# Scores of the last queries in two 64x64 array tiles, and identity transposes on TensorE in the first steps of a fused attention and MLP kernel

## Chip, cores, metric

One core of one Trainium2 chip. The time is device microseconds of a whole execution, median of several executions. The kernel before takes 1509.5 us in the runs taken with the change. All runs quoted are of the fast state.

## The reference

```python
# threshold attention: q, k, v (8, 8, 576, 64), tau = 0.02
scores = np.matmul(q, k.transpose(0, 1, 3, 2)) / 8
thresh = np.max(scores, axis=-1, keepdims=True) - tau
scores = np.where(scores >= thresh, scores, -1e9)
attn = softmax(scores)
x = np.matmul(attn, v)                  # then (B,H,S,D) -> (4608, 512)
# MLP: w_in (512, 2048), w_out (2048, 512)
h = x @ w_in
out = np.maximum(h, 0) ** 2 @ w_out
```

All data are float32. Two heads of one batch are handled together as a pair, 64 head dimensions each, so a pair fills 128 partitions. The 576 queries of a head are four blocks of 128 and a rest of 64.

## The kernel before

One pair and one block of queries make a *step*. Step s computes scores (TensorE), their maximum (VectorE), the exponentials (ScalarE), the threshold (VectorE) and the division (GpSimd). Step s+1 transposes the weights of step s on TensorE (`turn`; in the last 8 of the 20 visits to a pair VectorE and DMA do it instead), and later steps multiply them with v (`mix`). MLP matmuls (`h`, `o`) are spread between steps from step 13 on. In the first 13 steps (`early()`) there is no such filling yet, and the MLP's weights are loaded and rounded.

For the rest of 64 queries (`i == NBLK`) both heads are put in one matmul on the whole array: `qmid` holds the queries of head 0 in one corner, those of head 1 in the other, zeros elsewhere.

```python
# prep(), part 0: q of a pair has been transposed
    if part == 0 and NBLK in visits[n][1]:
        for u in range(2):
            rows = slice(u * D, (u + 1) * D)
            nc.gpsimd.tensor_copy(out=qmid[n % 2][rows, u * D:(u + 1) * D], in_=qT[rows, NBLK * P:S])

def scores(vis, i):
    n = 2 if i < NBLK else 1
    sc = [psum.tile([P, 2, 512], FP32, tag=f"s{u}", name=f"s{u}") for u in range(n)]
    halves = [(half, u) for half in range(2) for u in range(n)]
    if early():
        halves.sort(key=lambda x: x[1])
    for half, u in halves:
        if i < NBLK:      # 64 x 128 tile of the array, head u in its half of the rows
            rows, lhsT = slice(u * D, (u + 1) * D), qT[u * D:(u + 1) * D, i * P:(i + 1) * P]
        else:             # whole array
            rows, lhsT = slice(0, P), qmid[vis % 2]
        nc.tensor.matmul(sc[u][:, half, 0:HALF], lhsT, kT[rows, half * HALF:(half + 1) * HALF], start=True, stop=True)
    # ... maximum, bias (tensor_scalar), thr (tensor_scalar), z on VectorE

# the loop over steps, cut
        scores(n, i)
        ...                          # exponents, rounding stages 1 and 2, prep of the next pair
        if s in mixes:
            mix(*mixes[s])
        ...
        fill(quarter)                # MLP matmuls; nothing in the early steps
        for part in range(3):
            turn(*steps[s - 1], part)
            if on and part == 0:
                threshold(n, i)
            if on and part == 1:
                divide(n, i)         # two tensor_scalar on GpSimd
            fill(quarter)
        if on:
            if now:
                end_rounding(now[0]) # one addition on GpSimd, then the next weight load
```

Of the kernel before, what the change touches and what calls it, by code (L numbers as in the profile page):

```python
# [9 lines left out]
FP32 = mybir.dt.float32  # L10
# [9 lines left out]
def kernel(  # L20
# [10 lines left out]
    nc = tc.nc  # L31
    B, H, S, D = q.shape
    d_model, d_ff = moe_w_in.shape
    n_tokens = out.shape[0]
    P = 128
    HP = H // 2
    NPAIR = B * HP
    NBLK = S // P
    REST = S - NBLK * P
    HALF = S // 2  # L40
# [9 lines left out]
    const = ctx.enter_context(tc.tile_pool(name="const", bufs=1))  # L50
    pool = ctx.enter_context(tc.tile_pool(name="work", bufs=2))
    psum = ctx.enter_context(tc.tile_pool(name="psum", bufs=1, space=bass.MemoryType.PSUM))

    ident = const.tile([P, P], FP32, name="ident")
# [9 lines left out]
    wT = const.tile([P, NC9, S], FP32, name="wT")  # L64

    vs = [const.tile([P, 2 * NBLK + 2, D], FP32, name=f"vs{i}") for i in range(2)]
    qmid = [const.tile([P, P], FP32, name=f"qmid{i}") for i in range(2)]
    for i in range(2):
        nc.gpsimd.memset(vs[i], 0.0)
        nc.gpsimd.memset(qmid[i], 0.0)  # L70



# [22 lines left out]
    def load_weights(i):  # L96
        nc.sync.dma_start(out=weight_area(i).bitcast(mybir.dt.int64), in_=weight_piece(i)[0])
# [29 lines left out]
    def load_qk(n):  # L127


        b, h = divmod(visits[n][0], HP)  # L130
        h *= 2
        tiles = []
        for name, t in (("ql", q), ("kl", k)):
            x = pool.tile([P, S // 32, 32], FP32, tag=name, name=name)
            for m in range(4):
                src = t[b, h + m // 2, :, (m % 2) * 32:(m % 2) * 32 + 32].rearrange("(c p) d -> p c d", p=32)
                last = REST // 32 if t is k and m >= 2 else 0
                to = x[m * 32:(m + 1) * 32, :, :]
                nc.sync.dma_start(out=to[:, last:, :], in_=src[:, 0:S // 32 - last, :])  # L139
                if last:  # L140
                    nc.sync.dma_start(out=to[:, 0:last, :], in_=src[:, S // 32 - last:, :])
            tiles.append(x)
        loaded[n] = tiles

    def load_v(n):
        b, h = divmod(visits[n][0], HP)
        h *= 2
        t = vs[n % 2]
        for u in range(2):
            at = u * (NBLK + 1)  # L150
            nc.sync.dma_start(out=t[:, at:at + NBLK, :],
                              in_=v[b, h + u, 0:NBLK * P, :].rearrange("(c p) d -> p c d", p=P))
            nc.sync.dma_start(out=t[u * D:(u + 1) * D, at + NBLK, :], in_=v[b, h + u, NBLK * P:S, :])

    def prep(n, part):

        if part == 0:
            ready[n] = [pool.tile([P, S], FP32, tag="qT", name="qT"), pool.tile([P, S], FP32, tag="kT", name="kT")]
        qT, kT = ready[n]
        nc.vector.transpose((qT, kT)[part], loaded[n][part].rearrange("p c d -> p (c d)"))  # L160
        if part == 0 and NBLK in visits[n][1]:
            for u in range(2):
                rows = slice(u * D, (u + 1) * D)
                nc.gpsimd.tensor_copy(out=qmid[n % 2][rows, u * D:(u + 1) * D], in_=qT[rows, NBLK * P:S])

    weights = {}

    def scores(vis, i):

        qT, kT = ready[vis]  # L170
        n = 2 if i < NBLK else 1
        sc = [psum.tile([P, 2, 512], FP32, tag=f"s{u}", name=f"s{u}") for u in range(n)]
        halves = [(half, u) for half in range(2) for u in range(n)]
        if early():
            halves.sort(key=lambda x: x[1])
        for half, u in halves:
            if i < NBLK:
                rows, lhsT = slice(u * D, (u + 1) * D), qT[u * D:(u + 1) * D, i * P:(i + 1) * P]
            else:
                rows, lhsT = slice(0, P), qmid[vis % 2]  # L180
            nc.tensor.matmul(sc[u][:, half, 0:HALF], lhsT, kT[rows, half * HALF:(half + 1) * HALF],  # L181
                             start=True, stop=True)
        st = pool.tile([P, 7, 2], FP32, tag="st", name="st", bufs=4)
        mx, bias, thr, z = (st[:, j, 0:n] for j in range(4))
        for u in range(n):
            nc.vector.tensor_reduce(out=mx[:, u:u + 1], in_=sc[u][:, :, 0:HALF], axis=AX.XY, op=ALU.max)  # L186
        nc.vector.tensor_scalar(out=bias, in0=mx, scalar1=-SCALE, scalar2=None, op0=ALU.mult)  # L187
        nc.vector.tensor_scalar(out=thr, in0=mx, scalar1=ntau8, scalar2=None, op0=ALU.add)


        nc.vector.tensor_tensor(out=z, in0=thr, in1=mx, op=ALU.is_gt)  # L191
        w = pool.tile([P, n, S], FP32, tag="w", name="w", bufs=3)
        weights[vis, i] = w, sc, st

    def exponents(vis, i):
        w, sc, st = weights[vis, i]
        for u in range(len(sc)):
            nc.scalar.activation(out=w[:, u, :].rearrange("p (h k) -> p h k", h=2), in_=sc[u][:, :, 0:HALF],  # L198
                                 func=AF.Exp, bias=st[:, 1, u:u + 1], scale=SCALE)
# [137 lines left out]
    visits = [(g, list(range(FIRST))) for g in range(HP)] + [(g, list(range(FIRST, NBLK + 1))) for g in range(HP)]  # L337
# [4 lines left out]
    def by_dma(n):  # L342

        return n >= 3 * HP
# [24 lines left out]
    def early():  # L369
        return state["step"] < min(chunk_at)  # L370

    def add_chunk(j):
        waiting.extend((IN_US, mlp_in, j, f, x) for f in range(NFT) for x in range(2))
        waiting.extend((OUT_US, mlp_out, j, t, x) for t in range(TCH // P) for x in range(NFT // OF))
# [14 lines left out]
    def fill(us):  # L389
        state["left"] += us  # L390
        while waiting and state["left"] >= waiting[0][0] / 2:
            cost, fn, *what = waiting.popleft()
            state["left"] -= cost
            fn(*what)
# [3 lines left out]
    for s, (n, i) in enumerate(steps):  # L398
        if s <= min(chunk_at) - 2:
            x = int(visits[n][1].index(i) != 1)  # L400
        else:
            x = 2 if n >= 2 * HP and i == NBLK else 1
# [5 lines left out]
    def end_rounding(p):  # L408
        round_weights(p, 3)
        if p + RAW < n_pieces:  # L410
            load_weights(p + RAW)

    load_qk(0)
    load_v(0)
    for i in range(RAW):
        load_weights(i)
    for part in range(2):
        prep(0, part)
    done = 0
    for s in range(END + 1):  # L420
        state["step"] = s
        on = s < NST
        now = []
        if on:
            n, i = steps[s]
            at = visits[n][1].index(i)
            now = list(range(done, done + pieces[s]))
            done += pieces[s]
            more = n + 1 < len(visits)
            short = len(visits[n][1]) <= FIRST  # L430
            if at == (0 if short else 1) and more:
                load_qk(n + 1)
            if now:
                round_weights(now[0], 0)
            scores(n, i)
            if now or early():
                exponents(n, i)
            if now:
                round_weights(now[0], 1)
                round_weights(now[0], 2)  # L440
            if short and at == 1 and more:
                prep(n + 1, 0)
                prep(n + 1, 1)
        if s in mixes:
            mix(*mixes[s])
        for j in chunk_at.get(s, ()):
            add_chunk(j)
        if 0 < s <= NST and by_dma(steps[s - 1][0]):
            m, x = steps[s - 1]
            turn_blocks(m, x)  # L450
            if x % 2 or x == NBLK:
                place_blocks(m, x // 2)
        quarter = rate(s) / 4 if s < END else 1e9
        fill(quarter)
        for part in range(3):
            if 0 < s <= NST and not by_dma(steps[s - 1][0]):
                turn(*steps[s - 1], part)
            if on and part == 0:
                if not (now or early()):
                    exponents(n, i)  # L460
                threshold(n, i)
            if on and part == 1:
                divide(n, i)
            fill(quarter)
        if on:
            if now:
                end_rounding(now[0])
            for p in now[1:]:
                for stage in range(3):
                    round_weights(p, stage)  # L470
                end_rounding(p)
            if not short and at == 3 and more:
                prep(n + 1, 0)
                prep(n + 1, 1)
            if more and at == len(visits[n][1]) - 1:
                load_v(n + 1)
# [32 lines left out]
```

## Time and profile before

| | before |
|---|---|
| median, lowest to highest of 4 | 1509.5 us, 1509.1 to 1509.7 |
| TensorE busy, of a span of 1507.6 us | 1443.9 us, 5504 instructions |
| 0 to 43, 43 to 107, 107 to 250 us: TensorE busy | 55, 75, 83% |
| from 250 us on | 99.7%, clock 1.00 |
| first h, first o | 107.0, 246.7 us |

A float32 matmul stands as two instructions in the trace, a transpose as one.

### The profile page before, as it was taken

Reading aid. Unit: us, or ns where it says so; the run is one execution under the profiler, and the core shown is the slowest. Engines: PE = TensorE matmul, PEld = TensorE weight load, DVE = VectorE, ACT = ScalarE, POOL = GpSimd, SP = SyncE. Lnnn points to the kernel's source line nnn. Section 1 sums busy time; section 2 is a strip of 40 time slices with the busy share of each in tenths; the row PEclk is TensorE's granted clock in tenths of the full one; section 3 lists DMA queues with packets and bytes.
Section 4 is the critical chain, followed back from the end, with each engine's and each line's share of the span. In section 5 each row is a group of like instructions: output and inputs, shape, how many; then the busy total and the mean of one; then the engine's idle time right before and its main releaser. Section 6 shows DMA issues by size and latency. Waiting matters only on the chain.

```text
span 1507.6 us, 17982 instructions
## 1 busy us (share of the span) xinstructions
PE 1443.9 (96%) x5504; PEld 756.2 (50%) x5504; DVE 824.8 (55%) x2049; ACT 414.4 (27%) x789; POOL 488.1 (32%) x619
## 2 busy tenths in 40 slices
PE   4788888999999999999999999999999999999998
PEld 3445445455455455455455455455455455455453
DVE  5779887346566665555556566565656565520000
ACT  3445554232122222122123122122223122111010
POOL 3456666124124233133133234133133223221020
PEclk9879989999999999999999999999999999999999
DMA  6345332114554454454554454444554454430000
GB/s 146 90 109 133 100 98 49 38 31 76 98 97 87 94 93 87 86 96 87 99 105 79 91 95 84 88 95 85 99 101 83 88 97 81 85 70 7 15 0 21
DMA packets 520255, 123.02 MB, mean 82 GB/s; under 512 B 511456, under 2 KB 511456, under 8 KB 520160
## 3 DMA queue, kind: packets, MB, share of 16 engines
q1 hardware_dynamic: 520128, 121.88, 41.6%
q8 instruction: 45, 0.74, 0.2%
q14 instruction: 50, 0.41, 0.1%
q0 software_dynamic: 32, 0.00, 0.0%
HBM read 48.63 MB, written 9.44 MB: 39 GB/s over the span
## 4 chain that ended last, share of the span: by engine, by line
PE 91%; DVE 6%; SPq 1%; issue 1%; ACT 0%; DMA 0%; DVEq 0%; ACTq 0%
PE o L326 34%; PE h L311 33%; PE s L181 13%; PE x_ps L289 11%; DVE st L186 2%; PE w_ps L229 1%; DVE cv L117 1%; DVE w L209 1%; SPq L139 1%; DVE cv L119 1%; DVE cv L116 1%; DVE st L187 0%; DVE st L191 0%; DVE kT L160 0%; ACT w L198 0%
## 5 line engine op out<-in xcount | busy, mean ns | idle before, releaser
L311 PE MATMUL h<-xT,w_in_sb 128*128 128x384 f32 x1536 | 523.8, 493 | 0.0
L326 PE MATMUL o<-w_out_sb,g 128*128 128x512 f32 x1152 | 515.3, 597 | 0.0
L186 DVE TENSOR_REDUCE st<-s 128x1 f32<-128x576 f32 x288 | 207.2, 753 | 394.9 <-PE s L181 394.9
L218 POOL TENSOR_SCALAR w<-w,st 128x576 f32<-128x576 f32 x288 | 233.9, 821 | 518.3 <-DVE st L212 499.3
L311 PEld LDWEIGHTS h<-xT,w_in_sb 128*128 128x128 f32 x1536 | 286.1, 191 | 205.2 <-issue 28.6
L326 PEld LDWEIGHTS o<-w_out_sb,g 128*128 128x128 f32 x1152 | 213.0, 190 | 256.8 <-issue 251.8
L316 POOL TENSOR_TENSOR g<-g 128x384 f32<-128x384 f32 x192 | 158.4, 826 | 375.7 <-ACT g L315 374.4
L198 ACT ACTIVATE w<-s,st 128x576 f32<-128x576 f32 x288 | 199.7, 742 | 272.3 <-DVE st L187 211.0
L209 DVE SCALAR_TENSOR_TENSOR w<-s,st,w 128x576 f32<-128x576 f32 x288 | 222.2, 804 | 57.5 <-ACT w L198 57.5
L181 PE MATMUL s<-kT,qT 64*128 64x288 f32 x1024 | 180.1, 453 | 39.5 <-DVE w L209 31.1
L315 ACT ACTIVATE g<-h 128x384 f32<-128x384 f32 x192 | 94.4, 492 | 323.5 <-PE h L311 323.4
L289 PE MATMUL x_ps<-wT,vs 128*64 128x320 f32 (+3 forms) x1280 | 174.9, 421 | 0.0
L181 PEld LDWEIGHTS s<-kT,qT 64*128 64x128 f32 x1024 | 101.2, 196 | 130.9 <-issue 96.7
L256 DVE STREAM_TRANSPOSE wb<-w 128x576 f32<-128x576 f32 x216 | 156.3, 757 | 17.7 <-DMA wT<-wb 9.7
L289 PEld LDWEIGHTS x_ps<-wT,vs 128*64 128x64 f32 x1280 | 88.3, 140 | 81.7 <-issue 34.9
L293 ACT COPY xT<-x_ps 128x256 f32<-128x256 f32 x48 | 17.9, 372 | 236.7 <-PE x_ps L289 236.7
L330 ACT COPY osb<-o 128x512 f32<-128x512 f32 x36 | 21.1, 587 | 176.9 <-PE o L326 98.7
L121 POOL TENSOR_TENSOR cv<-cv 128x512 f32<-128x512 f32 x32 | 40.8, 1274 | 78.0 <-DVE cv L119 65.7
L229 PE MATMUL w_ps<-ident,w 128*128 128x128 f32 x288 | 48.8, 306 | 7.1 <-ACT wT L230 6.9
L229 PEld LDWEIGHTS w_ps<-ident,w 128*128 128x128 f32 x288 | 37.8, 156 | 34.1 <-issue 13.9
L230 ACT COPY wT<-w_ps 128x384 f32<-128x384 f32 x96 | 42.4, 488 | 26.0 <-PE w_ps L229 25.9
L181 PE MATMUL s<-kT,qmid 128*128 128x288 f32 x128 | 37.6, 417 | 2.4 <-DVE w L209 2.4
(36 smaller groups left out, 457.8 us busy)
## 6 DMA issues: line engine op xcount, KB each, us to landing
wT<-wb SPq DMA_DIRECT2D x768, 72.0 KB, 2.2
ql<-in_q_dram SPq DMA_DIRECT2D x144, 72.0 KB, 2.5
vs<-in_v_dram SPq DMA_DIRECT2D x72, 128.0 KB, 2.5
out_dram<-osb SPq DMA_DIRECT2D x36, 256.0 KB, 2.2
area<-in_moe_w_in_dram SPq DMA_DIRECT2D x16, 512.0 KB, 3.9
area<-in_moe_w_out_dram SPq DMA_DIRECT2D x16, 512.0 KB, 3.6
kl<-in_k_dram SPq DMA_DIRECT2D x72, 72.0 KB, 2.5
kl<-in_k_dram SPq DMA_DIRECT2D x72, 64.0 KB, 2.3
```

The source lines that it names most:

```text
L181: nc.tensor.matmul(sc[u][:, half, 0:HALF], lhsT, kT[rows, half * HALF:(half + 1) * HALF], start=True, stop=True)
L186: nc.vector.tensor_reduce(out=mx[:, u:u + 1], in_=sc[u][:, :, 0:HALF], axis=AX.XY, op=ALU.max)
L198: nc.scalar.activation(out=w[:, u, :].rearrange("p (h k) -> p h k", h=2), in_=sc[u][:, :, 0:HALF], func=AF.Exp, bias=st[:, 1, u:u + 1], sc ...
L209: nc.vector.scalar_tensor_tensor(out=wu, in0=sc[u][:, :, 0:HALF], scalar=thr[:, u:u + 1], in1=wu, op0=ALU.is_ge, op1=ALU.mult, accum_out=s ...
L218: nc.gpsimd.tensor_scalar(out=w[:, u, :], in0=w[:, u, :], scalar1=z[:, u:u + 1], scalar2=rcp[:, u:u + 1], op0=ALU.add, op1=ALU.mult)
L229: nc.tensor.transpose(ps[:, n, :], w.rearrange("p u k -> p (u k)")[:, c * P:(c + 1) * P], ident)
L256: nc.vector.transpose(wb[:, u * KB:(u + 1) * KB, i % 2, :], w[:, u, :].rearrange("p (k q) -> p k q", q=32))
L289: nc.tensor.matmul(ps[u * D:(u + 1) * D, 0:nq], vs[n % 2][:, u * (NBLK + 1) + c, :], wT[:, cw, cols], start=(c == 0), stop=(c == NBLK))
L311: nc.tensor.matmul(h, w_in_sb[:, c, f * P:(f + 1) * P], xT[:, c, at:at + TCH], start=(c == 0), stop=(c == NMC - 1))
L315: nc.scalar.activation(out=g, in_=h, func=AF.Relu)
L316: nc.gpsimd.tensor_tensor(out=g, in0=g, in1=g, op=ALU.mult)
L326: nc.tensor.matmul(o, gs[j, f][:, t * P:(t + 1) * P], w_out_sb[:, f, :], start=(f == 0), stop=(f == NFT - 1))
```

## The change

It has two intents. The remaining queries need no copies into `qmid` and no multiplications with zeros, if each head's 64 queries use a 64x64 tile of the array, the two tiles side by side. And TensorE, half idle in the early steps, is kept at work with transposes of the identity so that its clock stays up.

```diff
-    qmid = [const.tile([P, P], FP32, name=f"qmid{i}") for i in range(2)]
...
-        if part == 0 and NBLK in visits[n][1]:
-            for u in range(2):
-                rows = slice(u * D, (u + 1) * D)
-                nc.gpsimd.tensor_copy(out=qmid[n % 2][rows, u * D:(u + 1) * D], in_=qT[rows, NBLK * P:S])
...
-        halves = [(half, u) for half in range(2) for u in range(n)]
+        halves = [(half, u) for half in range(2) for u in range(2)]
...
-            if i < NBLK:
-                rows, lhsT = slice(u * D, (u + 1) * D), qT[u * D:(u + 1) * D, i * P:(i + 1) * P]
-            else:
-                rows, lhsT = slice(0, P), qmid[vis % 2]
-            nc.tensor.matmul(sc[u][:, half, 0:HALF], lhsT, kT[rows, half * HALF:(half + 1) * HALF],
-                             start=True, stop=True)
+            rows = slice(u * D, (u + 1) * D)
+            to = sc[u] if i < NBLK else sc[0][rows]
+            nc.tensor.matmul(to[:, half, 0:HALF], qT[rows, i * P:min((i + 1) * P, S)],
+                             kT[rows, half * HALF:(half + 1) * HALF], start=True, stop=True)
...
+    def keep_busy(times):
+        idle = psum.tile([P, 4, P], FP32, tag="mm", name="idle", bufs=2)
+        for x in range(times):
+            nc.tensor.transpose(idle[:, x % 4, :], ident, ident)
+
     load_qk(0)
     load_v(0)
+    keep_busy(24)
...
         fill(quarter)
+        if 0 < s and early():
+            keep_busy(8)
         for part in range(3):
...
             fill(quarter)
+        if early():
+            keep_busy(8)
```

More of the change, by code (lines that the diff above doesn't have):

```diff
@@ L66 @@
     vs = [const.tile([P, 2 * NBLK + 2, D], FP32, name=f"vs{i}") for i in range(2)]
-    qmid = [const.tile([P, P], FP32, name=f"qmid{i}") for i in range(2)]
     for i in range(2):
         nc.gpsimd.memset(vs[i], 0.0)
-        nc.gpsimd.memset(qmid[i], 0.0)
     WP = 512
```

## The prediction

> **What bounds the kernel now.** I read the page first (busy shares and the 40 slices), then the busy time by stretches, the chain in order of time, and TensorE's timeline around single score groups.
>
> ```profile
> 0.00:43.00 43.00, 23.51 (x77) 15.39 (x79) 26.27 (x66) 14.89 (x26) 16.93 (x25) 1.00 0.62 141
> 43.00:107.00 64.00, 47.87 (x224) 28.58 (x221) 48.75 (x126) 31.81 (x62) 31.23 (x33) 0.76 0.42 98
> 107.00:250.00 143.00, 118.80 (x618) 69.84 (x617) 117.94 (x265) 77.29 (x157) 94.38 (x102) 0.92 0.42 105
> 250.00:1507.00 1257.00, 1253.72 (x4590) 642.38 (x4588) 631.84 (x1596) 290.39 (x546) 345.57 (x460) 1.00 0.41 76
> ```
>
> Columns: stretch, length, then busy us (instructions) of PE, PEld, DVE, ACT, POOL, then granted clock, DMA share, GB/s. There are two regimes. After 250 us PE is busy throughout at full clock: every added nanosecond of PE lengthens the run. Up to 107 us (the first 13 steps, where the code's `early()` holds for all but the last one) nobody is full, and the clock averages 0.76 in the second stretch. The 1.00 of the first stretch is no measurement: the clock's first record starts near 42.8 us, and the durations before it are those of half clock.
>
> ```profile
> 30.32 2.27 PE s L181 x6
> 32.61 1.51 DVE st L186 x2
> 35.07 0.70 DVE cv L117
> 36.23 0.74 DVE w L209 x2
> 37.11 3.00 PE s L181 x8
> 40.10 4.74 PE x_ps L289 x20
> 44.84 1.16 PE w_ps L229 x9
> 46.00 1.18 PE s L181 x8
> 47.20 1.43 DVE st L186 x2
> ```
>
> The chain (start, length) shows a ring: scores, maximum (L186), rounding and threshold on DVE, next scores, because the score buffers exist once. Scores cost 3.00 us cold and 1.18 warm; a plain step lasts 6.8 us cold (30.32 to 37.11), of which 2.3 us is the wait until head 0's scores are there, and 5.7 us warm. Where the ring meets a value product (x_ps), the link runs through PE alone.
>
> **What the Trainium skill says.** (1) "TensorE: Matmul & The Clock Gate", Part 1: half clock by default, full after about 3.4 us of busy time, half again after an idle window. The trace agrees and is sharper: all changes lie on one grid of 3.413 us (42.84, 53.08, 63.32, 73.56 ...). Every rise follows a window at least 0.88 full of matmuls; I divided PE's time in each window by line. (2) Same page, Part 4: a PE-mode transpose "doesn't count as PE-busy the same way". The trace agrees for the rise: the windows 73.56:76.97 and 94.04:97.45 were 100% busy, 1.74 and 1.30 us of that transposes (L229), and the clock stayed at 0.50. It disagrees for holding: 169.13:172.55 was busy for 1.64 us, 1.30 of them with transposes, and stayed warm, while 49.67:53.08, busy for 1.46 us and all of it matmuls, went cold. (3) "TensorEngine Tiling (Array Packing)", Key Properties: changing the tiling mode drains TensorE. The trace agrees; next fence. (4) Same page, Gotcha 1: different row tiles cannot write one PSUM bank at the same time. The matmuls of L241, in exactly the two diagonal 64x64 tiles and one bank, start 7 ns apart and leave 155 ns to the next, which is one 64-column slot (about 55 ns) and the switch: side by side works.
>
> ```profile
> 477.75 1.13 PE L181 MATMUL s<-kT,qmid 128*128 128x288 f32 x4
> 478.73 1.78 PE L311 MATMUL h<-xT,w_in_sb 128*128 128x384 f32 x5
> ...
> 411.60 1.24 PE L181 MATMUL s<-kT,qT 64*128 64x288 f32 x8
> 412.77 5.42 PE L326 MATMUL o<-w_out_sb,g 128*128 128x512 f32 x12
> 418.11 1.24 PE L181 MATMUL s<-kT,qT 64*128 64x288 f32 x8
> ```
>
> Start to start, four qmid instructions (two matmuls, an FP32 one counts twice) take 0.98 us, 243 ns each, and the h before and after keep their 322 ns. Eight tiled ones are four pairs, ideally 0.97 us too, but take 1.17; and twelve o between two tiled groups take 5.34 us instead of 12 x 0.429 = 5.15. So a visit to tiled mode costs 0.20 + 0.19 = 0.39 us on top.
>
> **Part 1: remaining queries in two tiles.** It removes 64 copies to qmid (15 us of POOL, not in the chain) and two memsets, and nothing from PE: two 128-row matmuls become two side-by-side pairs of equal streaming, four slots of 243 ns either way. The zero half of qmid cost no time. It adds the mode switch. Instruction by instruction the trace gives its four pieces: the last untiled instruction +94 ns (322 to 416), the first pair +104 with 128 weight columns but +50 with 64 columns (x_ps: 366 to 316), the last pair +97, the first untiled one after +104 (429 to 533). With 64 columns: 94 + 50 + 97 + 104 = 345 ns. After 250 us there are 26 such groups, 24 between untiled matmuls and 2 next to x_ps, which already pay one border (94 + 50 = 145 ns extra): 24 x 0.345 + 2 x 0.145 = 8.6 us, all on the path as PE is full. The other six lie before 250 us, where about half of PE's work is in the chain: 6 x 0.345 x 0.5 = 1.0 us. Sum: **+9.6 us**.
>
> **Part 2: the identity.** 24 transposes at the start, then 8 before and 8 after the transposes of w in steps 1 to 12. One takes 109 ns warm and 213 cold, start to start. The first 24 end by about 1.5 + 24 x 0.213 = 6.6 us, before the first scores at 8.45: free. They should not raise the clock, by (2). Then, by step:
> - Cold steps become PE-bound: scores 2.23 + 8 x 0.213 and a border 1.76 + nine w transposes 1.92 + eight more 1.70 + border 0.2 = 7.8 us against 6.8. Step 1 to 2: 2.93 + 1.76 + 1.92 + 1.70 + 0.2, so scores 2 start at 24.85, not 23.52. Scores 3 at 32.65 (before 30.32), scores 4 at 40.45 (37.11).
> - Step 4: scores to 42.7, x_ps cold until a window full of matmul ends, on the old grid 46.25; the remaining 4.5 pair slots of 0.32 end at 47.8, then 0.93 + 0.98 + 0.97 for the transposes. Scores 5 at 50.7, before 45.9: 4.8 us late.
> - From there the clock should hold: transposes fill what is idle. Plain steps last 5.7 us (DVE), value-product steps 2.0 + 3.4 + 0.93 + 0.98 + 0.97 = 8.3 us (PE, with 1.9 us of it identity). Scores 8 at 50.7 + 5.7 + 5.7 + 8.3 = 70.4 (before 66.9), 11 at 90.1 (87.6), 13 at 101.5 (100.1).
> - Step 13 then runs warm: 1.2 + 3.4 us instead of 2.2 + 4.4. Its x_ps ends near 106.2, before at 106.6. Sum: **-0.4 us**.
>
> The rest is paced by steps and follows this point one to one, so 1509.5 + 9.6 - 0.4 = 1518.7; I say **1518**, taking off a little for an early rise and for POOL relief.
>
> **Rivals.** (a) The identity also raises the clock, so all early steps are warm. Scores 2 still wait for the second k (landing near 21.9 us), so they start at 23.1; then 5.7, 5.7, 8.3 and so on put scores 13 at 93.8 and the end of its x_ps at 98.4, 8.2 us early: 1511. For it: pure transposes in a window were never seen. Against: the two full windows that stayed cold. (b) The identity neither raises nor holds. Then most steps stay at 7.8 us and more, and the 1.9 us of each PE-bound step comes on top; step by step the end of x_ps falls near 118.5, 12 us late: 1531. Against: the window 169.13:172.55, which transposes kept warm. (c) The diagonal tiles run one after the other: another 4 x 243 ns in each of 26 groups, 25 us: 1543. Against: L241. (d) Tiles without the cost of switching, with part 2 as I have it: 1509. Against: every tiled group in the trace pays it.
>
> **Range and chances.** I give my main course 0.65, (a) 0.15, (b) 0.1, the others and mixtures 0.1. The free grid and the five short cold spells between 107 and 250 us may move by some us either way. That gives 1510 to 1527. Two per cent are 30 us: faster 0.01, same 0.96, slower 0.03.
>
> **What would show it.** Right: score groups of remaining queries with 8 instructions, about 1.12 us from first to next start, 0.1 us more on each neighbour; the stretch from the first h (before 107 us) to the end some 9 us longer; no cold record between about 46 and 107 us; steps 2 to 4 later than before by 1.3 to 3.3 us, the first h within 2 us of before. A first h near 98 us would mean (a), one near 118 (b). Pairs of L181 243 ns apart instead of some 7 would mean (c). The number is wrong if the switch into 64x64 differs from that of L241, or if the early steps have a releaser that I took for hidden, such as a copy on ACT that frees the buffer of the identity.

## The result and the profile after

The changed kernel took 1524.15 us (1523.04 to 1525.02 in 4 executions), the kernel before 1509.51. The ratio is 1.0097, with a 95% interval of 1.0079 to 1.0114. Ratios here are the mean time of one kernel's fast runs over that of the other's of the same rounds, so not quite the ratio of the medians quoted. The sign and the class were foretold ("same": under 2%), and the range of 1510 to 1527 holds; the number was 6 us low.

Where the 13.7 us of the two traces lie is read from two marks. The first `h` came at 112.06 us instead of 107.01: 5.05 us are lost in the early steps. From the first `o` (251.85, before 246.72) to TensorE's last instruction it took 1265.57 us instead of 1257.01: 8.56 us more. Between the two marks nothing changed (139.79 and 139.71 us).

The same stretches as before, in the changed kernel:

```profile
0.00:43.00 43.00, 31.01 (x168) 23.19 (x169) 29.57 (x68) 14.88 (x26) 16.68 (x23) 0.88 0.60 141
43.00:107.00 64.00, 53.77 (x337) 38.36 (x337) 45.61 (x114) 30.78 (x60) 27.08 (x28) 0.89 0.38 84
107.00:250.00 143.00, 119.37 (x640) 67.88 (x639) 118.64 (x266) 75.21 (x152) 92.03 (x89) 0.91 0.47 111
250.00:1520.00 1270.00, 1267.42 (x4716) 635.74 (x4714) 635.96 (x1603) 293.45 (x551) 340.15 (x414) 1.00 0.41 75
```

In the second line the clock rose from 0.76 to 0.89 and PE is busier, yet DVE, whose work here is fixed, did only 45.6 us of it in the 64 us, where it had done 48.8. The clock went up and the steps went slower. The last stretch is full, as before.

TensorE's timeline around one group of remaining queries, now in tiles:

```profile
357.20 1.13 PE L304 MATMUL h<-xT,w_in_sb 128*128 128x384 f32 x3
358.26 1.19 PE L174 MATMUL s<-kT,qT 64*64 64x288 f32 x8
359.38 1.88 PE L304 MATMUL h<-xT,w_in_sb 128*128 128x384 f32 x5
```

Start to start the group takes 1.12 us (1.118 in the mean of 26 groups, before 0.977). Instruction by instruction the four pairs take 293, 243, 242 and 339 ns, the second of each pair 6 or 7 ns behind the first; the `h` ahead grew from 322 to 416 and the one behind to 427. These are the four pieces of the prediction.

The chain of work in two early steps of the changed kernel, 6 and 7:

```profile
51.37 1.25 PE s L174 x5
52.65 1.50 DVE st L179 x2
54.34 1.20 DVE st L181
...
57.32 0.75 DVE w L202 x2
58.11 3.02 PE s L174 x8
61.13 5.39 PE x_ps L282 x20
66.52 1.02 PE idle L410 x8
67.55 0.98 PE w_ps L222 x9
68.53 0.87 PE idle L410 x8
```

Scores at 51.37 are warm (1.25 us to the first head's end), those at 58.11 are cold again (3.02 us), and so is the value product behind them (5.39 us). Then 16 identity transposes follow in TensorE's own chain. And a tiny tensor_scalar, L181, on two columns, takes 1.20 us of the chain. Each of these has its own experiment below.

Where the early steps stood (start of the scores in us, from the traces). The last column is a run with the identity alone, described below:

| scores of step | before | predicted | changed | identity alone, low group |
|---|---|---|---|---|
| 2 | 23.5 | 24.9 | 23.5 | 23.3 |
| 4 | 37.1 | 40.5 | 35.9 | 35.8 |
| 5 | 45.9 | 50.7 | 45.8 | 44.0 |
| 8 | 66.9 | 70.4 | 69.3 | 64.4 |
| 11 | 87.6 | 90.1 | 93.1 | 84.9 |
| 13 | 100.1 | 101.5 | 105.5 | 97.3 |

Steps 1 to 4 came earlier than foretold, the steps with a value product (4, 7, 10: from one score to the next 9.8, 11.2, 11.4 us in the changed kernel) much later.

### The profile page after: what moved, and what is told of

Its sections match the earlier page's. It is cut to its first block, busy times and chain, and to the rows that moved or that the text cites. A ratio compares the mean times of both kernels' runs of the same rounds, so it can differ in the third digit from the quotient of the medians.

```text
span 1521.3 us, 18622 instructions
## 1 busy us (share of the span) xinstructions
PE 1471.6 (97%) x5856; PEld 765.2 (50%) x5856; DVE 829.8 (55%) x2049; ACT 414.3 (27%) x789; POOL 475.9 (31%) x553
## 4 chain that ended last, share of the span: by engine, by line
PE 92%; DVE 5%; SPq 1%; issue 1%; ACT 1%; DMA 0%; DVEq 0%; ACTq 0%
PE o L319 33%; PE h L304 33%; PE s L174 13%; PE x_ps L282 11%; DVE st L179 1%; PE w_ps L222 1%; DVE cv L115 1%; SPq L137 1%; DVE w L202 1%; DVE cv L117 1%; PE idle L410 1%; DVE cv L114 0%; DVE st L180 0%; ACT w L191 0%; DVE kT L158 0%
## 5 line engine op out<-in xcount | busy, mean ns | idle before, releaser
L174 PE MATMUL s<-kT,qT 64*128 64x288 f32 (+1 forms) x1280 | 211.6, 436 | 27.0 <-DVE w L202 25.3
L174 PEld LDWEIGHTS s<-kT,qT 64*128 64x128 f32 (+1 forms) x1280 | 112.6, 179 | 142.8 <-issue 88.0
L282 PE MATMUL x_ps<-wT,vs 128*64 128x320 f32 (+3 forms) x1280 | 178.8, 428 | 0.0
L249 DVE STREAM_TRANSPOSE wb<-w 128x576 f32<-128x576 f32 x216 | 156.3, 758 | 17.7 <-DMA wT<-wb 11.2
L222 PE MATMUL w_ps<-ident,w 128*128 128x128 f32 x288 | 42.3, 276 | 7.1 <-ACT wT L223 6.9
L222 PEld LDWEIGHTS w_ps<-ident,w 128*128 128x128 f32 x288 | 33.7, 142 | 26.7 <-issue 12.0
L181 DVE TENSOR_SCALAR st<-st,ntau 128x2 f32<-128x2 f32 (+1 forms) x160 | 39.2, 245 | 0.0
```

What stands on the lines that cost most here:

```text
L174: nc.tensor.matmul(to[:, half, 0:HALF], qT[rows, i * P:min((i + 1) * P, S)], kT[rows, half * HALF:(half + 1) * HALF], start=True, stop=True)
L222: nc.tensor.transpose(ps[:, n, :], w.rearrange("p u k -> p (u k)")[:, c * P:(c + 1) * P], ident)
L249: nc.vector.transpose(wb[:, u * KB:(u + 1) * KB, i % 2, :], w[:, u, :].rearrange("p (k q) -> p k q", q=32))
L282: nc.tensor.matmul(ps[u * D:(u + 1) * D, 0:nq], vs[n % 2][:, u * (NBLK + 1) + c, :], wT[:, cw, cols], start=(c == 0), stop=(c == NBLK))
```

## The experiments

Theory: the tiles cost 8.6 us by changing the mode of the array, and the early steps lose 5 us for other reasons. Rivals: the tiles are cheap, or the identity helps and all is the tiles. Each kernel ran beside the kernel before on the same chip.

### 1. The tiles alone

```diff
-    keep_busy(24)            # and both keep_busy(8) in the loop
```

> The kernel before with the change's tiles for the remaining queries alone, no identity. Theory (every visit to the tiled mode costs TensorE 0.345 us where it is full: 24 groups x 0.345 + 2 x 0.145 = 8.6 us after 250 us, about 1 us before): 1509.5 + 9.6 = 1519, between 1518 and 1520; first h within 1 us of the kernel before (107.0). Rival (the tiles' cost is small and the identity shifts the rest): under 1512.

Measured: 1517.95 us (1516.51 to 1519.16, 5 executions), the kernel before 1509.82 beside it, ratio 1.0052 (1.0040 to 1.0064). A loss of 8.1 us by the medians. From first `o` to the end 1265.58 us, as in the changed kernel. The tiles' share after 250 us is confirmed; the 1 us that I had put on the six early groups isn't there (first `h` to first `o`: 139.58 us). So the total falls just below the 1518 to 1520 that I expected. The first `h`, expected within 1 us of 107.0, came at 105.70: the clock was up for one window from 21.00 us on, without any identity.

### 2. The identity alone

```diff
     # kernel before, qmid kept
+    keep_busy(24)            # and both keep_busy(8) in the loop
```

> The kernel before with the change's identity transposes alone, qmid kept. Theory (the early steps lost 5 us, the tiles the other 8.6): 1514.5, between 1513 and 1516; first h near 112, as in the changed kernel, and the time from the first h to the end as before (1396.7 us in the trace). Rival (the identity helps as intended and the whole loss is the tiles): 1509 or less.

Measured: 1510.09 us in the median, but in two groups: 1504.51, 1505.03, 1505.26 and 1514.92, 1517.03, 1517.14. Neither expectation holds. The identity gains 5 us or loses 5 to 7 us by the execution, with the same program. The profiled execution was one of the low group, and its chain at the same step 7 reads:

```profile
56.28 1.97 PE s L181 x7
58.25 3.38 PE x_ps L289 x20
61.63 1.02 PE idle L417 x8
```

Here scores and product are warm: 1.97 and 3.38 us, in place of 3.02 and 5.39. From these scores to the next it took 8.16 us, where the prediction had 8.3.

What differs between this trace and that of the changed kernel is read from the clock in windows of 3.413 us, the grid on which all changes of clock lie. First the changed kernel, profiled in the slower of the two courses:

```profile
17.38:20.80 3.42, 3.42 (x14) 2.52 (x13) 2.03 (x7) 0.32 (x1) 2.86 (x3) 0.50 0.73 103
20.80:24.21 3.41, 2.92 (x24) 2.57 (x23) 2.98 (x7) 3.30 (x7) 0.00 (x0) 1.00 0.50 155
54.93:58.34 3.41, 1.52 (x13) 1.29 (x12) 3.24 (x8) 2.01 (x5) 1.45 (x2) 1.00 0.70 111
58.34:61.76 3.42, 3.42 (x11) 1.86 (x11) 2.12 (x6) 0.00 (x0) 2.79 (x4) 0.50 0.49 153
61.76:65.17 3.41, 3.41 (x14) 1.39 (x12) 3.32 (x9) 1.37 (x2) 0.46 (x1) 0.50 0.00 0
```

And the identity alone, in its good execution:

```profile
52.33:55.75 3.42, 2.07 (x19) 1.83 (x17) 3.23 (x7) 2.50 (x5) 1.46 (x3) 1.00 0.78 123
55.75:59.16 3.41, 2.88 (x14) 1.78 (x16) 3.11 (x9) 0.00 (x0) 2.77 (x4) 1.00 0.58 174
```

In both, TensorE rests for 1.9 us at the end of step 6. In the first, the whole rest lies within one window: 1.52 us busy of 3.41, and the next window is cold. In the second the grid cuts the rest in two: 2.07 us busy, and the clock holds. That the grid makes the two groups is argued from this, not shown: no kernel was profiled in both of its courses. And the rest alone does not decide. In the run of experiment 4 the same rest, 1.93 us up to the scores at 35.99, lay wholly in one window with 1.49 us busy, and the clock held:

```profile
32.62:36.03 3.41, 1.49 (x15) 1.25 (x13) 3.24 (x9) 2.50 (x5) 1.32 (x2) 1.00 0.74 115
36.03:39.45 3.42, 3.42 (x18) 2.02 (x20) 3.12 (x8) 0.38 (x1) 2.79 (x4) 1.00 0.56 163
```

The first two lines of the changed kernel, further up, show a rise behind a window of which 1.48 us were identity transposes. This alone proves nothing for the identity, as the tiles alone rose at 21.00 us too; the window with nothing but identity does (last section).

### 3. The changed kernel again

> The changed kernel as it is, five more executions. The identity alone fell into two groups (three executions near 1505, three near 1515 to 1517), and its trace from the low group held the clock without a break from 21.6 us on. Theory (the throttle's 3.41 us grid lies by chance in each execution; where it puts the 1.9 us pause of a plain step into one window, the clock drops before each product): the changed kernel has two groups too, 8 us above: near 1513 and 1523 to 1525; its first four executions were all of the upper one. Rival (in the changed kernel the drop is fixed, by the tiles or otherwise): all within 1522 to 1526 again.

Measured: 1512.70 and 1512.76, and four executions from 1524.65 to 1524.83. Two groups, as the theory expected; with the first four executions that makes two of ten in the low one. Both groups lie about 8 us above those of the identity alone (1512.7 against 1504.9; 1524.4 against 1516.4, means). So the two groups are not tied to the tiles, and the tiles' cost is the same in both.

### 4. No identity where a value product runs

```diff
-        if 0 < s and early():
+        if 0 < s and early() and s not in mixes:
...
-        if early():
+        if early() and s not in mixes:
```

> As the identity alone, but without its 16 transposes in the three early steps with a value product (4, 7, 10), where they sit in TensorE's own chain. Theory (there each costs its full time: 1.9 us per step at full clock): 3 x 1.9 = 5.7 us less than the identity alone, so about 1509, as the clock still drops before these steps. Rival (what costs is only that these steps begin cold, the identity rides along): no change, 1514.

Measured: 1504.82 us (1501.81 to 1506.97), ratio 0.9960 to the kernel before. It beats the identity alone by 5.3 us in the medians and 2.7 in the best executions; as that run has two groups, the size can't be taken from the total, and the 1509 expected was 4 us too high. From the trace: steps 4 and 10 now last 6.55 us where the identity alone, warm, has 8.16. The 16 transposes cost 1.6 us of each warm product step, not 1.9. Step 7 lost the clock here and took 8.07 us.

### 5. More identity in plain steps

```diff
-            keep_busy(8)
+            keep_busy(8 if s in mixes else 14)     # the second call, behind turn
```

> As the identity alone, but with 14 instead of 8 transposes after those of w in the plain early steps, which fill 0.65 us of the 1.9 us that TensorE then still idles. Theory (the clock drops where less than about half of a 3.41 us window is busy; in the changed kernel the windows before the drops had 0.41, 0.45 and 0.45 busy, these will have 0.6 or more): no drop before the products of steps 7, 10 and 13, which then take 8.3 us instead of 11.2 and 11.4, and step 13 1.5 us less; with step 4 about 8 us less than the identity alone, 1506 to 1508. Rival (transposes don't hold the clock, only matmuls do): drops as before, 1514 or a little more.

Measured: 1506.45 us (1505.48 to 1507.40), one group, ratio 0.9976. Its trace has the clock at full from 22.97 us to 190 us. As the theory has it, none of the five executions is in the high group, with 0.65 us of additional transposes in the pause. The bound of about half a window in that theory is not sound, though: it left out the drop of the changed kernel at 37.86 us, behind a window busy for 1.94 of 3.41 us, 0.57 (below, in experiment 6). Compared with the low group of the identity alone it is 1.5 us slower, as scores 2 came at 24.57 us instead of 23.33, behind the six transposes more in the cold step 1.

### 6. Both, with qmid

```diff
+        if 0 < s and early() and s not in mixes:
+            keep_busy(8)
...
+        if early() and s not in mixes:
+            keep_busy(8 if s < 2 else 14)
```

> The kernel before with qmid, and the identity only in plain early steps (none where a value product runs), 14 of them instead of 8 after those of w from step 2 on. Theory (both losses of the early part are removed: the pauses are too short for a cold window in any position of the grid, and no identity stands in the products' chain): no drop from about 23 us on in any execution, so one group, a spread of under 3 us, median 1500 to 1502. Rival (the two savings are the same time): about the better of the two, 1505.

Measured: 1503.68 us (1501.05 to 1505.34), ratio 0.9958. That is not told apart from experiment 4 (0.9960, both intervals within 0.9946 to 0.9972), and 2.8 us below experiment 5 in the medians. The spread is 4.3 us, the median lies above the 1500 to 1502 expected, and the profiled execution, the slowest of the five, still lost the clock twice in these steps. The expectation on that point failed:

```profile
53.08:56.49 3.41, 2.20 (x12) 1.46 (x10) 3.11 (x9) 0.47 (x2) 1.81 (x2) 1.00 0.63 99
56.49:59.90 3.41, 3.41 (x11) 1.24 (x12) 3.29 (x7) 0.95 (x2) 2.31 (x3) 0.50 0.40 137
```

A window with 2.20 us busy went cold, while one with 2.07 us held in experiment 2. In this one 1.79 us were scores and 0.41 identity; in that one no scores at all, only transposes. The changed kernel has such a pair in one trace:

```profile
34.45:37.86 3.41, 1.94 (x10) 1.33 (x10) 3.11 (x9) 1.36 (x4) 1.95 (x2) 1.00 0.66 160
48.10:51.52 3.42, 1.94 (x18) 1.70 (x17) 3.21 (x10) 2.76 (x6) 0.79 (x1) 1.00 0.29 80
```

The first, all scores but for 0.04 us, was followed by half clock, and the product of step 4 began cold; the second, 1.04 us identity and 0.92 transposes of w, held. So the busy share alone doesn't order the windows: early scores, whose two heads start 0.74 us apart and for a time fill half of the array each, seem to count for less than transposes. That reading is argued, not tested.

### 7. and 8. GpSimd's addition first, or short

In steps 3, 6, 9 and 12 the tensor_scalar of L180 or L181 took 1.2 to 1.3 us. VectorE and GpSimd in the changed kernel, step 6:

```profile
54.17 0.17 DVE L180 TENSOR_SCALAR st<-st 128x2 f32<-128x2 f32 x1
...
54.22 1.28 POOL L121 TENSOR_TENSOR w_in_sb<-cv 128x512 f32<-128x512 f32 x1
54.25 1.28 DVE L181 TENSOR_SCALAR st<-st,ntau 128x2 f32<-128x2 f32 x1
```

The tensor_scalar ends (55.53) when GpSimd's addition ends (55.50). In the kernel before, step 3, the cold scores had delayed VectorE just so long that it came when GpSimd was done (34.26):

```profile
33.00 1.26 POOL L123 TENSOR_TENSOR w_in_sb<-cv 128x512 f32<-128x512 f32 x1
...
34.14 0.17 DVE L187 TENSOR_SCALAR st<-st 128x2 f32<-128x2 f32 x1
34.22 0.22 DVE L188 TENSOR_SCALAR st<-st,ntau 128x2 f32<-128x2 f32 x1
```

The Trainium skill, "SBUF — State Buffer", Who interferes with whom, says that a tensor_scalar of VectorE in its two-port mode and GpSimd share a pair of ports, and that whoever comes first keeps it for its whole instruction while the other "fully blocks". These lines fit that: 1.28 us in place of 0.22, up to the end of the addition. The mode of the instruction itself is not in the trace. Two kernels test it, both on top of experiment 6. One changes GpSimd's order:

```diff
             if on and part == 1:
+                if now and early():
+                    end_rounding(now[0])
                 divide(n, i)
...
-            if now:
+            if now and not early():
                 end_rounding(now[0])
```

> As the run before in this list, but with GpSimd's addition for the weights ahead of its two divisions in the early steps, not behind. Theory (in the steps after a rounding, 3, 6, 9 and 12, a tiny tensor_scalar of VectorE lasted 1.28 us, until GpSimd's addition ended: both want one SBUF port, and this takes the time back that warm scores had won): VectorE is then held until the divisions end, about 0.5 us earlier, so these four steps last 6.2 instead of 6.75 us: 2 us less. Rival (VectorE waited for something else at that place): no change, within 0.7 us.

The other makes the addition short, with a wrong result:

```diff
+            few = slice(0, 16) if early() else slice(0, WP)
-            nc.gpsimd.tensor_tensor(out=weight_piece(i)[1], in0=t, in1=d, op=ALU.add)
+            nc.gpsimd.tensor_tensor(out=weight_piece(i)[1][:, few], in0=t[:, few], in1=d[:, few], op=ALU.add)
```

> As the one with the identity in plain steps only, but GpSimd's addition for the weights covers 16 of 512 columns in the early steps (a wrong result on purpose; the weights' tile is set to zero at the start by GpSimd). Theory (port shared by VectorE and GpSimd): steps 3, 6, 9 and 12 last 5.7 us instead of 6.75 and the tensor_scalars there about 0.2 us: 4 us less. Rival (something else held VectorE): no change, within 0.7 us.

Measured: 1499.81 us (1497.05 to 1500.12), ratio 0.9932, for the order; 1496.87 us (1495.11 to 1497.35), ratio 0.9916, for the short addition. Steps 6, 9 and 12 last 6.2 us in the first and 5.7 in the second, in place of 6.75, both as expected from the port; step 3, expected to shrink alike, took 6.65 us in the first and 5.7 in the second. The short addition in the trace:

```profile
49.21 0.17 DVE L189 TENSOR_SCALAR st<-st 128x2 f32<-128x2 f32 x1
...
49.25 0.22 POOL L125 TENSOR_TENSOR w_in_sb<-cv 128x16 f32<-128x16 f32 x1
49.28 0.22 DVE L190 TENSOR_SCALAR st<-st,ntau 128x2 f32<-128x2 f32 x1
```

Both gained more than expected (3.9 and 6.8 instead of 2 and 4 us by the medians). With shorter steps TensorE's pauses are shorter too, and neither trace has a drop between 21.5 and 123 us, while that of experiment 6 had two, each of which cost about 1.5 us (steps 7 and 10: 8.1 instead of 6.55 us). How often the executions without a trace drop is not known.

### 9. The same order in the kernel before, without identity

> The kernel before with GpSimd's addition ahead of its divisions in the early steps, and nothing else. Theory (at half clock VectorE waits for the scores while GpSimd adds, so the shared port costs little there: the first tiny tensor_scalar of each step took 3.61 us in 14 early steps, 1.2 us more than 14 x 0.17): up to 1.2 us faster than the kernel before, 1508 to 1510. Rival (the order on GpSimd is worth its 4 us with or without a warm clock): 1505 to 1506.

Measured: 1508.45 us (1507.27 to 1509.14), the kernel before 1509.24, ratio 0.9996 (0.9981 to 1.0010): no difference that the runs resolve. The order is worth something only when warm scores bring VectorE to that place early.

### 10. Into the tiled mode twice

```diff
     for half, u in halves:      # on top of the tiles alone
+        if i == NBLK and (half, u) == (1, 0):
+            nc.tensor.transpose(between[:, 0, 0:P], ident, ident)
```

> The tiles alone, as in the first of these runs, with one transpose of the identity on the whole array between the two halves of each group of remaining queries: the group leaves the tiled mode and enters it a second time. Theory (the cost is that of changing the mode): per group 97 ns for leaving + 109 for the transpose with 60 and 94 at its two borders + 50 for entering = 0.41 us; 26 groups where TensorE is full make 10.7 us, and the six early ones up to 1: 11 to 12 us more than the tiles alone, 1529. Rival (the cost is that of having eight instructions where there were four): only the transposes themselves, 26 x 0.11 = 3 us more, 1521.

Measured: 1531.93 us (1531.37 to 1533.83), ratio 1.0154 to the kernel before. The group after 250 us grew from 1.118 to 1.524 us, 0.407 where 0.41 was expected, and first `o` to the end from 1265.6 to 1276.2 us, 10.6 where 10.7 was expected:

```profile
356.82 0.70 PE L177 MATMUL s<-kT,qT 64*64 64x288 f32 x4
357.46 0.33 PE L173 MATMUL between<-ident 128*128 128x128 f32 x1
357.72 0.70 PE L177 MATMUL s<-kT,qT 64*64 64x288 f32 x4
```

One transpose, which takes 109 ns among its like, here holds TensorE for 260 ns, and the pairs beside it pay too. So it is the change of mode that costs, not the number of instructions. The remaining 3.2 us lie between first `h` and first `o` (142.80 us), more than the 1 us expected for the six groups there. They need not be the split's: the traces of experiment 6 and of the short addition, without tiles, have 142.3 and 142.1 us there too, the eleven others 139.3 to 140.0. What sets the two values is not known.

### 11. and 12. Without the start; with the tiles

```diff
-    keep_busy(24)               # from experiment 7
```

> As the run with GpSimd's addition first, without the 24 transposes at the start. Theory (they raise the clock at 4 to 7 us, but it is lost again by about 14 us, before scores 2, and rises for good near 21 us through step 1 in any case): no change, within 1 us, near 1499. Rival (the early rise is worth something): 1501 or more.

Measured: 1499.12 us (1497.75 to 1499.81), ratio 0.9935 (0.9922 to 0.9949). The 24 transposes at the start do nothing that counts. With experiment 7, from which it can't be told apart, this is the fastest correct kernel; it beats the kernel before by 0.65% and the changed one by more.

The last one is experiment 7 with the tiles in place of qmid.

> The changed kernel (with tiles) with the identity in plain steps only, 14 after the transposes of w from step 2 on, and GpSimd's addition first. Theory (the parts add up: the tiles cost 8 us where TensorE is full, whatever the early steps do): 1499.5 + 8 = 1507.5, between 1506.5 and 1508.5, in one group. Rival (the tiles are worth their cost in a faster early part): 1504 or less.

Measured: 1507.08 us (1506.77 to 1508.50), as the sum has it: 7.3 us by the medians over experiment 7, where the tiles alone cost 8.1.

## Why the prediction was right, and where it was wrong

- **The tiles in the full part.** "Sum: +9.6 us", of which 8.6 after 250 us: right. The trace has 8.56, the tiles alone 8.1 in total. The pieces were read from other groups of the same kernel, and all four came out within 2 ns. The term of 1.0 us for the six groups before 250 us was too large; it measured about 0.
- **Side by side.** Right: pairs of L174 start 6 to 7 ns apart, in one bank. Rival (c) is out.
- **"They should not raise the clock"**: wrong. The window from 3.73 to 7.14 us, 3.02 us of identity and nothing else, was followed by a rise (lost again at 13.97 us), and from 20.80 to 37.86 us the clock was up, so that scores 4 came at 35.9 us, not 40.5. I had two windows in the trace of before, half matmul, half transposes of w, that stayed cold, and blamed the transposes. They are no evidence: the changed kernel's window from 58.34 to 61.76 us is full too, 2.79 us scores and 0.70 value product with no transpose, and stayed cold (experiment 2, the clock in its last line), and the run with the tiles alone has mixed windows with a rise behind them and others without. In all 14 traces, up to 400 us, 20 cold windows were full and stayed cold, eight of them without a transpose. What they lack is open; that scores on half of the array's rows count less, as in experiment 6, would fit.
- **"From there the clock should hold: transposes fill what is idle"**: this is the step that failed most. They run as soon as TensorE reaches them, and are done 1.9 us before the scores can go on. They don't lie where the pause is. In both traces of the changed kernel, of its high group, windows that hold the pause went cold, and steps 7 and 10, with a value product, took 11.2 to 11.5 us instead of 8.3. That the same happened in the other six high executions of it, and in the three of experiment 2, is concluded from their times.
- **"Plain steps last 5.7 us (DVE)"**: right for steps 2, 5, 8 and 11 (5.6 to 5.7 us), wrong for 3, 6, 9 and 12 (6.7 to 6.9 us). VectorE, being earlier, ran into GpSimd's addition. Four times 1.05 us: most of what the warm scores won went there. The chain and the waits of the kernel before named neither, though its L187 took 3.61 us in 14 early steps where 14 x 0.17 are 2.4.
- **"Sum: -0.4 us"** for the identity: as a mean of the two groups fair (1510.65 against 1509.8 us beside it), but no execution is there: 5 us less or 5 to 7 more. The 1518 of the prediction lies between the two groups of the changed kernel, 1512.7 and 1524; its range held both. The first four executions happened to fall into the upper one. The two groups were not foreseen, so that the early steps' share kept the total within the range is partly luck.
- **Slips in the working**, without weight for the result: `early()` holds for all of the first 13 steps (0 to 12), step 13 is the fourteenth; the 8 transposes behind those of w run in step 0 too; and rival (a) adds up to 93.6 us for scores 13, not 93.8.

## What to carry to other kernels

A matmul in array tiles between matmuls on the whole array pays for changing the mode twice, here 0.35 us in all, and zeros multiplied in the whole array cost nothing here, as the moving stream was equally long (four slots of 243 ns either way): compare streams and borders, not arithmetic. Work that is to keep a clock up did so best here where it shortened the pause (1.9 us to 1.22 in experiment 5), and it cost its full time where it stood ahead of work in the chain (1.6 us per product step). When one engine gets faster, look at what the next one will meet there: here VectorE met GpSimd at a shared port, and moving one GpSimd instruction gave back half of what the meeting cost (steps of 6.2 us; 6.75 with it, 5.7 without).

## What the Trainium skill lacked or had wrong

- "TensorE: Matmul & The Clock Gate", Part 4, has it that transposes don't count as busy for the clock in the same way, and that full clock does not engage for them. Here the clock rose behind a window that held only identity transposes, 3.02 us of 3.41:

```profile
3.73:7.14 3.41, 3.02 (x15) 2.62 (x13) 1.00 0.82 120
```

  (TensorE's time by the identity's line alone in the changed kernel, clock in the third place from the end; here the 1.00 stands for a time before the clock's first record, the rise is the record at 7.14 us.)
- The same page, Part 1, names an idle window of about 3.4 us as what brings the clock down, and knows frequent shorter pauses as a cause, but without a size. Here single pauses of 1.9 us were enough: windows with 1.52 us of 3.41 busy went cold. And busy time alone doesn't order them: 2.20 us, mostly staggered scores, went cold, 1.49 and 2.07 us, nearly all transposes, held.
- The same page, Part 1, notes that the grid runs free and puts the warm-up that depends on it under 1% of a kernel. It does not say that executions of one program can fall into groups later on: here two, 12 us apart (1512.7 and 1524.7). That is 0.8%, within the page's bound, and yet more than either part of the change; that the grid parts them is argued (experiment 2).
- "TensorEngine Tiling (Array Packing)", Key Properties, says that a change of mode drains TensorE but gives no size: 94 ns on the instruction ahead, 50 (64 weight columns) or 104 ns (128) on the first pair, 97 on the last, 104 behind.
- The same page, Gotcha 1, says that different row tiles can't use the same PSUM bank at one time. The two diagonal 64x64 tiles wrote one bank in different partitions with starts 7 ns apart and 243 ns per pair, with correct results.
